# Polysketch attention and a mixture of experts: the expert stage in written order, with conditionals behind block 34

## The chip, the cores and the metric

The kernel runs on one core of a Trainium2 chip. The core has five engines with instruction queues of their own: TensorE (PE; its weight loads are listed as PEld), VectorE (DVE), ScalarE (ACT), GpSimd (POOL) and SyncE (SP). The metric is the time of one execution on the device in microseconds (us), as the median of several runs.

## What is computed

```python
# attention: phi(x) = (S1 x) (S2 x)^T, flattened
q_p, k_p = (phi(q), phi(k))                       # 4 batches, 4 heads, 1088 rows, 32 wide
kv = np.einsum('bhsf,bhsd->bhfd', k_p, v)
z = np.sum(k_p, axis=2)
x = einsum(q_p, kv) / (einsum(q_p, z) + 1e-06)    # -> x: 4352 tokens of 128
# mixture of experts behind two gates: 4 groups of 4 experts
g_idx = np.argmax(x @ w_group, axis=1)            # a token's group, weight g_w
e_idx = np.argmax(xg @ w_expert[g], axis=1)       # its expert in the group, weight e_w
h = np.maximum(xg[mask_e] @ w1[g, e], 0.0)        # 128 -> 1024
ye = h @ w2[g, e]                                 # 1024 -> 128
out[tok_idx] = (g_w * e_w)[:, None] * ye
```

The inputs come from a random generator with a fixed seed.

## The kernel before

The program has four stages. The first two read the keys and values and then the queries, and write the tokens x to DRAM as `x_d`. The third (routes) finds each token's expert and weight and sorts the tokens by expert into blocks of 128 slots: a block belongs to one expert, so an expert with 200 tokens takes two blocks. Any routing fits into `NBLK` = 49 blocks, and 34 is the least that 4352 tokens can fill. The routing leaves four tables in SBUF: `idx_g` (the row of `x_d` to fetch for each slot; 0 for an empty slot), `idx_s` (the row of the output to write; out of range for an empty slot, so that nothing is written), `wslot` (a slot's weight) and `bex` (a block's expert). `last` holds how many blocks end at each expert, so its last entry is the count of blocks that hold a token.

The fourth stage, on which the change bears, runs over all 49 blocks b, filled or not. For each block:

- `first_layer(b)`, lines 650 to 669: POOL gathers 128 rows of `x_d` into `xg` (an indirect DMA, L652). PE and DVE load the block's expert number from `bex` into a register (L655). DVE copies that expert's first weights out of `W1` into `w1b` (L658). PE transposes `xg` into PSUM (`pt`, L660) and DVE copies it to `xb` (L662). PE multiplies by the 8 pieces of `w1b` into `ph` (L665); in fp32 the trace shows two passes for each piece, 16 in all. ACT applies the relu and writes `hT` (L668).
- `second_layer(b)`, lines 671 to 682: PE multiplies the 8 pieces of `hT` by the expert's second weights into `py` (L674), again 16 passes, each piece with a register instruction before it (ISA in the lists below). DVE scales by `wslot` into `yo` (L678). POOL scatters `yo` to the output rows (an indirect DMA, L680). Since the rows are known only at run time, each scatter waits until the one before has landed.

The loop is written with the first layer one block ahead of the second. The order on each engine, however, is not the written one: the scheduler of the programming layer reorders the instructions by its own model of time, and buffers are handed out from pools (`xg` 4 buffers, `w1b`, `xb`, `hT`, `yo` 3, the PSUM tiles 2). The scheduler also splits the eight pieces of `py` around other work on PE.

Of the kernel before, what the change touches and what calls it, by code (L numbers as in the profile page):

```python
"""Polysketch attention, then a mixture of experts behind two gates: one core, one launch.

The reference's attention runs in float64 (its sketches S1, S2 come in float64), and its
quotient num / den is large just where den cancels. The chip's widest type is fp32, so den is
computed in parts: an operand is cut into bf16 slices on a fixed grid, products of slices are
summed on the tensor engine within 24 bits, and the sums of one order stay apart until the end.
  den[t] = sum_i a[t, i] c[t, i],  a = S1 q,  c = N q,  N = S1 G (S2^T S2),  G = sum_s k_s k_s^T
The numerator, the quotient and the experts are in fp32.

Tokens are then sorted by expert into blocks of 128 slots. NBLK blocks hold any routing. A  # L10
block picks its expert's weights, which stay in SBUF, by a register.
"""

# [9 lines left out]
F32 = mybir.dt.float32  # L23
BF16 = mybir.dt.bfloat16
I32 = mybir.dt.int32
ALU = mybir.AluOpType
ACT = mybir.ActivationFunctionType
AX = mybir.AxisListType
ENG = mybir.EngineType
PSUM = bass.MemoryType.PSUM  # L30
# [5 lines left out]
DM = H * D  # L36
N = B * S
# [3 lines left out]
G, EG, DFF = 4, 4, 1024  # L41
NE = G * EG
FC = DFF // 128
NBLK = (N - NE) // 128 + NE
NL = G + NE
NS = 4
# [7 lines left out]
def segments(c):  # L54
    """Token tile c: (batch, first row, rows)."""
    out, t = [], 128 * c
    while t < 128 * (c + 1):
        b = t // S
        e = min(128 * (c + 1), S * (b + 1))
        out.append((b, t - 128 * c, e - t))  # L60
        t = e
    return out
# [3 lines left out]
def attention_then_moe(ctx: ExitStack, tc: tile.TileContext, qT_d, kT_d, kn_d, vn_d, sT_d, s2_d,  # L66
                       wr_d, w1_d, w2_d, out):
    nc = tc.nc
# [3 lines left out]
    x_d = dram.tile([N, DM], F32, name="x_d")  # L72

    def kept(name, shape, dt=F32):
        return keep.tile(shape, dt, name=name)

    ident = kept("ident", [128, 128])
# [3 lines left out]

# [1 line left out]
    sT_i = kept("sT_i", [128, 2 * R, 2], I32)  # L83
# [7 lines left out]
    def power_above(m, n, psum, name):  # L91
        """[128, n] of maxima by partition -> a power of two above each column's, everywhere."""
        t = psum.tile([128, 256], F32, name="pw_t", tag="small")
# [15 lines left out]
    def grid(out, in_, c):  # L109
        """in_ rounded to a multiple of the last bit of c."""  # L110
        nc.vector.tensor_scalar(out=out, in0=in_, scalar1=c, scalar2=c, op0=ALU.add,  # L111
                                op1=ALU.subtract)
# [10 lines left out]
    def slices(dst, hi, lo, r):  # L123
        """hi + lo, hi below 1 and lo below its last bit, cut into dst [p, NS, n]; r is scratch."""
        rest = hi
        for i in range(NS):
            grid(dst[:, i], rest, ROUND * WQ[i])
            if i < NS - 1:
                sub(r, rest, dst[:, i])
                rest = r  # L130
                if i == 1:
                    add(r, r, lo)

    def products(out, left, right):
        """Sums of slice products by order: out(i) views orders i.., right(n) the first n slices."""
        for i in range(NS):
            nc.tensor.matmul(out(i), lhsT=left(i), rhs=right(NS - i), start=(i == 0),  # L137
                             stop=(i == NS - 1), skip_group_check=True)

# [1 line left out]
    def decode(w, p, n, tag):  # L141
# [50 lines left out]

# [1 line left out]
    with ExitStack() as kctx:  # L194
# [37 lines left out]

        # The sketches' slices, below 1, and Bm = S2^T S2.
        m1 = tiny.tile([128, 1], F32, name="m1")
# [17 lines left out]
        def refine(orders, n, name):  # L252
            """orders, sums [128, n] by order -> slices of their sum over a power of two."""
            o = [kbig.tile([128, n], F32, name=f"o{i}_{name}") for i in range(len(orders))]
            for t, z in zip(o, orders):
                nc.vector.tensor_copy(out=t, in_=z)
            hi, lo, t, u = (kbig.tile([128, n], F32, name=f"{x}_{name}") for x in "hltu")
            # hi + lo is the sum, and hi its nearest fp32.
            add(hi, o[0], o[1])
# [10 lines left out]
            hi = t  # L270
# [78 lines left out]

        # N = S1 G Bm, transposed: Bm (G S1^T).  # L350
        Gs, p_g = refine([Go[:, i].rearrange("p b d -> p (b d)") for i in range(NS + 1)], B * 32, "g")
# [27 lines left out]

# [1 line left out]
    with ExitStack() as qctx:  # L381
# [3 lines left out]
        def features(c0):  # L385
            """The parts of den before their last sums, and phi(q)."""
            nt = min(4, NT - c0)
# [116 lines left out]

# [1 line left out]
    idx_g = kept("idx_g", [128, NBLK], I32)  # L506
    idx_s = kept("idx_s", [128, NBLK], I32)
    wslot = kept("wslot", [128, NBLK])
    bex = kept("bex", [1, NBLK], I32)
    with ExitStack() as rctx:  # L510
        rp = rctx.enter_context(tc.tile_pool(name="rp", bufs=1, reuse_waits="tile"))
# [24 lines left out]
        def gate(z, k):  # L536
            """One-hot of the first largest of 4 logits, and the sum of the exponentials."""
            top = T(f"gt{k}", [NT])
# [28 lines left out]

        # Tokens of the same expert before a token: in its tile, and in the tiles before.
        lower, ones16 = T("lower", [128], BF16), T("ones16", [128], BF16)
# [48 lines left out]

        # A block's expert: how many experts end at it or before.
        le, bf = rp.tile([1, NBLK, NE], F32, name="le"), rp.tile([1, NBLK], F32, name="bf")  # L620
# [4 lines left out]

        # A slot's token and weight: one-hots of its place and its block, multiplied.
        in_b, vals = T("in_b", [NT, NBLK]), T("vals", [NT, 2, NBLK])
# [17 lines left out]

# [1 line left out]
    mp = ctx.enter_context(tc.tile_pool(name="mp", bufs=3, reuse_waits="tile"))  # L647
    mps = ctx.enter_context(tc.tile_pool(name="mps", bufs=2, reuse_waits="tile", space=PSUM))

    def first_layer(b):  # L650
        xg = mp.tile([128, DM], F32, name="xg", bufs=4)
        nc.gpsimd.indirect_dma_start(  # L652
            out=xg, out_offset=None, in_=x_d,
            in_offset=bass.IndirectOffsetOnAxis(ap=idx_g[:, b:b + 1], axis=0))
        ev = nc.values_load(bex[0:1, b:b + 1], engines=[ENG.PE, ENG.DVE], min_val=0, max_val=NE - 1,  # L655
                            skip_runtime_bounds_check_because="at most NE - 1, by a minimum")
        w1b = mp.tile([128, DFF], F32, name="w1b")
        nc.vector.tensor_copy(out=w1b, in_=W1[:, ds(ev, 1), :].rearrange("p o f -> p (o f)"))  # L658
        pt = mps.tile([128, DM], F32, name="pt")
        nc.tensor.transpose(pt, xg, ident)  # L660
        xb = mp.tile([128, 128], F32, name="xb")
        nc.vector.tensor_copy(out=xb, in_=pt)  # L662
        ph = mps.tile([128, FC, 128], F32, name="ph")
        for f in range(FC):
            nc.tensor.matmul(ph[:, f], lhsT=w1b[:, 128 * f:128 * f + 128], rhs=xb, start=True,  # L665
                             stop=True)
        hT = mp.tile([128, FC, 128], F32, name="hT")
        nc.scalar.activation(out=hT, in_=ph, func=ACT.Relu)  # L668
        return ev, hT

    def second_layer(b, ev, hT):
        py = mps.tile([128, DM], F32, name="py")
        for f in range(FC):
            nc.tensor.matmul(py, lhsT=hT[:, f],  # L674
                             rhs=W2[:, ds(ev * FC + f, 1), :].rearrange("p o d -> p (o d)"),
                             start=(f == 0), stop=(f == FC - 1))
        yo = mp.tile([128, DM], F32, name="yo")
        nc.vector.tensor_scalar(out=yo, in0=py, scalar1=wslot[:, b:b + 1], scalar2=None,  # L678
                                op0=ALU.mult)
        nc.gpsimd.indirect_dma_start(  # L680
            out=out, out_offset=bass.IndirectOffsetOnAxis(ap=idx_s[:, b:b + 1], axis=0), in_=yo,
            in_offset=None, bounds_check=N - 1, oob_is_err=False)

    ahead = first_layer(0)
    for b in range(NBLK):
        mine = ahead
        if b + 1 < NBLK:
            ahead = first_layer(b + 1)
        second_layer(b, *mine)

# [42 lines left out]
```

## Time and profile before

| | us |
|---|---|
| median of 3 runs | 509.83 |
| lowest and highest run | 509.80, 511.18 |
| span of the profiled execution, first to last instruction | 507.7 |
| PE busy in it | 402.5 (79%) |
| POOL busy | 208.2 (41%) |
| DVE busy | 253.8 (50%) |
| ACT busy | 73.0 (14%) |
| expert stage, from the first transpose of a gathered tile to the end | 298.3 to 507.7 |

The span is the profiled execution's own time between its first and its last instruction; what a run takes beyond it lies around the program. All times below are counted from the start of the span. A line of the kernel is written L674; an arrow `out<-in` names the tiles; `x49` is a count. In a timeline and in the chain of waits each row begins with a start and a duration in us, and brackets tell how long the engine had been idle and who ended that. Rows with a q behind the engine's name (POOLq, PEldq) are instructions of its queue, such as waits, register loads and drains; their durations are in ns.

### The profile page before, as it was taken

How to read it: one execution, taken by the hardware profiler on the slowest of the kernel's cores; microseconds unless marked ns; L12 is line 12 of the kernel's file. 1: busy time of each engine (PE TensorE's matmuls, PEld its weight loads, DVE VectorE, ACT ScalarE, POOL GpSimd, SP SyncE). 2: the span in 40 equal slices, each digit the busy share in tenths (PEclk: the TensorE clock that was granted, in tenths of full speed). 3: DMA queues.
4: the chain of work that ended last, by engine and by line, in shares of the span. 5: the costliest groups of instructions: out<-in, count | busy, mean ns of one | idle time of the engine just before them, and what ended most of it. 6: DMA issues, size and time to landing. Idle time of an engine off the chain costs nothing.

```text
span 507.7 us, 7633 instructions
## 1 busy us (share of the span) xinstructions
PE 402.5 (79%) x2724; PEld 331.7 (65%) x2724; DVE 253.8 (50%) x772; ACT 73.0 (14%) x104; POOL 208.2 (41%) x262
## 2 busy tenths in 40 slices
PE   0347979925899989997730659999999999999990
PEld 0326767812535638575620649999999999999980
DVE  8798363567645566655469932333233322233310
ACT  1000000001011111110110002322223222322220
POOL 0463163001735666535410053555554555455420
PEclk9998688956656565556555669999999999999996
DMA  8990482097000000000100010111111111111100
GB/s 304 374 250 1 156 254 64 0 354 308 2 1 21 22 21 23 20 22 0 43 11 0 0 33 25 32 34 28 29 34 37 28 32 34 35 31 26 12 1 0
DMA packets 16547, 34.28 MB, mean 68 GB/s; under 512 B 2597, under 2 KB 6961, under 8 KB 16512
## 3 DMA queue, kind: packets, MB, share of 16 engines
q1 hardware_dynamic: 13376, 28.35, 16.5%
q0 software_dynamic: 3136, 5.45, 4.6%
q8 instruction: 23, 0.38, 0.3%
q14 instruction: 12, 0.10, 0.1%
HBM read 29.33 MB, written 5.44 MB: 68 GB/s over the span
## 4 chain that ended last, share of the span: by engine, by line
PE 63%; DVE 18%; issue 6%; POOL 6%; ACT 3%; DMA 2%; POOLq 0%; SPq 0%; ACTq 0%; DVEq 0%
PE ph L665 17%; PE py L674 16%; PE ab L448 8%; PE pnum L475 5%; PE py L137 4%; PE pg L303 3%; ACT hT L668 3%; PE pl L491 2%; PE slot L637 2%; POOL rk L298 2%; DVE ks L111 2%; PE px L486 1%; POOL rq L396 1%; DVE top_p_k L89 1%; DVE kp L324 1%
## 5 line engine op out<-in xcount | busy, mean ns | idle before, releaser
L674 PE MATMUL py<-W,hT 128*128 x784 | 107.1, 281 | 2.7 <-ACT hT L668 2.6
L674 PEld LDWEIGHTS py<-W,hT 128*128 128x128 f32 x784 | 94.9, 192 | 11.5 <-ACT hT L668 11.5
L665 PE MATMUL ph<-xb,w1b 128*128 128x128 f32 x784 | 97.9, 280 | 0.0
L665 PEld LDWEIGHTS ph<-xb,w1b 128*128 128x128 f32 x784 | 94.0, 197 | 0.1
L652 POOL DMA_INDIRECT xg<-x_d,idx_g x49 | 49.7, 1014 | 107.2 <-PE pt L660 58.4
L668 ACT ACTIVATE hT<-ph 128x1024 f32<-128x1024 f32 x49 | 50.2, 1025 | 177.8 <-issue 111.3
L658 DVE COPY w1b<-W 128x1024 f32 x49 | 34.4, 705 | 74.7 <-issue 52.2
L680 POOL DMA_INDIRECT out_dram<-yo,idx_s x49 | 49.5, 1011 | 36.6 <-issue 12.5
L448 PE MATMUL ab<-qT,SR 64*128 64x512 f32 (+1 forms) x72 | 54.3, 999 | 0.1
L678 DVE TENSOR_SCALAR yo<-py,wslot 128x128 f32<-128x128 f32 x49 | 17.2, 351 | 62.5 <-PE py L674 62.0
L303 PE MATMUL pg<-ks 128*128 128x512 bf16 (+3 forms) x144 | 33.1, 348 | 16.8 <-DVE ks L111 16.8
L137 PEld LDWEIGHTS <-qs 128*128 128x128 bf16 (+1 forms) x144 | 14.9, 137 | 34.8 <-DVE qs L111 12.0
L137 PE MATMUL py<-M,qs 128*128 128x256 bf16 (+6 forms) x144 | 25.0, 322 | 9.9 <-DVE qs L111 7.0
L475 PE MATMUL pnum<-KV,qp 128*128 128x64 f32 (+1 forms) x144 | 30.7, 395 | 0.0
L475 PEld LDWEIGHTS pnum<-KV,qp 128*128 128x128 f32 (+1 forms) x144 | 28.8, 304 | 2.3 <-issue 1.5
L396 POOL TENSOR_TENSOR rq<-qT,qs 128x512 f32<-128x512 f32 (+1 forms) x9 | 10.1, 1122 | 48.9 <-DVE qs L111 42.3
L303 PEld LDWEIGHTS <-ks 128*128 128x128 bf16 x144 | 14.7, 112 | 21.4 <-issue 18.6
L111 DVE TENSOR_SCALAR qs<-rq,CQ 128x512 bf16<-128x512 f32 (+1 forms) x27 | 17.1, 633 | 21.9 <-POOL rq L396 21.9
L298 POOL TENSOR_TENSOR rk<-rk,ks 128x1152 f32<-128x1152 f32 x8 | 19.6, 2446 | 19.2 <-DVE ks L111 7.1
L448 PEld LDWEIGHTS ab<-qT,SR 64*128 64x128 f32 x72 | 16.5, 297 | 12.4 <-issue 6.9
L637 PE MATMUL slot<-vals,place 128*128 128x98 f32 x68 | 10.2, 325 | 15.1 <-DVE vals L518 15.1
L298 POOL TENSOR_TENSOR rk<-kn,ks 128x1152 f32<-128x1152 f32 x4 | 10.1, 2520 | 29.3 <-DVE pw L98 16.6
(312 smaller groups left out, 497.3 us busy)
## 6 DMA issues: line engine op xcount, KB each, us to landing
W<-in_w_dram SPq DMA_DIRECT2D x4, 2048.0 KB, 13.7
kn<-in_kn_dram SPq DMA_DIRECT2D x4, 576.0 KB, 5.8
kT<-in_kT_dram SPq DMA_DIRECT2D x4, 576.0 KB, 6.8
vn<-in_vn_dram SPq DMA_DIRECT2D x4, 576.0 KB, 4.0
qT<-in_qT_dram SPq DMA_DIRECT2D x4, 544.0 KB, 11.5
x_d<-xt SPq DMA_DIRECT2D x8, 256.0 KB, 2.2
xg<-x_d,idx_g POOLq DMA_INDIRECT x49
out_dram<-yo,idx_s POOLq DMA_INDIRECT x49
```

The source lines that it names most:

```text
L111: nc.vector.tensor_scalar(out=out, in0=in_, scalar1=c, scalar2=c, op0=ALU.add, op1=ALU.subtract)
L137: nc.tensor.matmul(out(i), lhsT=left(i), rhs=right(NS - i), start=(i == 0), stop=(i == NS - 1), skip_group_check=True)
L298: nc.gpsimd.tensor_tensor(out=r, in0=rest, in1=ks[:, i], op=ALU.subtract)
L303: nc.tensor.matmul(pg[:, i:NS, :], lhsT=ks[:, i, c, :], rhs=ks[:, 0:NS - i, c, :], start=(c == 0 and i == 0), stop=(c == SC - 1 and i == N ...
L448: nc.tensor.matmul(ab[x][:, 0:w], lhsT=SR[rows, x].rearrange("p a x y -> p (a x y)"), rhs=qf[rows], start=True, stop=True)
L475: nc.tensor.matmul(pnum[r0:r0 + n, c, 64 * pr:64 * pr + 64], lhsT=qp[:, pr, cols], rhs=KV[:, b, pr, :], start=True, stop=True)
L652: nc.gpsimd.indirect_dma_start(out=xg, out_offset=None, in_=x_d, in_offset=bass.IndirectOffsetOnAxis(ap=idx_g[:, b:b + 1], axis=0))
L658: nc.vector.tensor_copy(out=w1b, in_=W1[:, ds(ev, 1), :].rearrange("p o f -> p (o f)"))
L665: nc.tensor.matmul(ph[:, f], lhsT=w1b[:, 128 * f:128 * f + 128], rhs=xb, start=True, stop=True)
L668: nc.scalar.activation(out=hT, in_=ph, func=ACT.Relu)
L674: nc.tensor.matmul(py, lhsT=hT[:, f], rhs=W2[:, ds(ev * FC + f, 1), :].rearrange("p o d -> p (o d)"), start=(f == 0), stop=(f == FC - 1))
L680: nc.gpsimd.indirect_dma_start(out=out, out_offset=bass.IndirectOffsetOnAxis(ap=idx_s[:, b:b + 1], axis=0), in_=yo, in_offset=None, bounds ...
```

## The change

The two functions of the expert stage become five (`gather`, `weights`, `turn`, `first_layer`, `second_layer`), and a `step(b)` calls them for blocks b + 4, b + 2, b + 1, b + 2 and b, in this order. The stage is traced inside a block that keeps the written order on every engine, with tiles that are used in fixed rotation (6 of `xg`, 3 of the other SBUF tiles, 2 of the PSUM tiles, as many PSUM tiles as before). Steps 0 to 33 stand in a straight line. Step 34 and each later one stands in a conditional `tc.If(used > b)`, and each conditional stands inside the one before, so that the first one that does not hold leaves all the rest out. `used` is the count of blocks that hold a token, copied to an integer by DVE and loaded into a register by all five engines. The docstrings and comments are dropped as well, and the other stages stay as they are.

```diff
+LOW = N // 128
+TAIL = 1
...
+    n_used = kept("n_used", [1, 1], I32)
...
+        nc.vector.tensor_copy(out=n_used, in_=last[0:1, NE - 1:NE])
...
+    xg, w1b = ring(mp, "xg", [128, DM], 6), ring(mp, "w1b", [128, DFF], 3)
+    xb, hT = ring(mp, "xb", [128, 128], 3), ring(mp, "hT", [128, FC, 128], 3)
+    yo = ring(mp, "yo", [128, DM], 3)
+    ph, pt = ring(mps, "ph", [128, FC, 128], 2), ring(mps, "pt", [128, DM], 2)
+    py = ring(mps, "py", [128, DM], 2)
...
+    def turn(b):
+        if b >= NBLK:
+            return
+        nc.tensor.transpose(pt(b), xg(b), ident)
+        nc.vector.tensor_copy(out=xb(b), in_=pt(b))
...
-    ahead = first_layer(0)
-    for b in range(NBLK):
-        mine = ahead
-        if b + 1 < NBLK:
-            ahead = first_layer(b + 1)
-        second_layer(b, *mine)
+    def step(b):
+        gather(b + 4)
+        weights(b + 2)
+        first_layer(b + 1)
+        turn(b + 2)
+        second_layer(b)
+
+    def rest(b):
+        with tc.If(used > b):
+            for c in range(b, b + TAIL):
+                step(c)
+            if b + TAIL < NBLK:
+                rest(b + TAIL)
+
+    with tc.manual_schedule():
+        used = nc.values_load(n_used, min_val=LOW, max_val=NBLK,
+                              skip_runtime_bounds_check_because="LOW to NBLK, by construction")
+        for b in range(4):
+            gather(b)
+        for b in range(2):
+            weights(b)
+            turn(b)
+        first_layer(0)
+        for b in range(LOW):
+            step(b)
+        rest(LOW)
```

PE in the middle of the stage, before. Here `ph_2976` is a block's first layer, and `hT_2985` is what ACT makes of it; `py_2987` belongs to the block before. Five pieces of `py_2987` stand between the two, of which the first row is shown:

```order
L665 MATMUL ph_2976<-xb_2974,w1b_2970 128x128 x8
L674 ISA
L674 MATMUL py_2987<-W2_134,hT_2948 128x128
L655 TENSOR_LOAD bex_2071
...
L660 MATMUL pt_3009<-ident_64,xg_3001 128x128
L674 ISA
L674 MATMUL py_3024<-W2_134,hT_2985 128x128
...
L665 MATMUL ph_3013<-xb_3011,w1b_3007 128x128 x8
```

The same place in the changed kernel, one step with its end and the start of the next (the number behind a name is its place in the rotation; all eight pieces of `py1` and of `py0` stand together, of which one is shown):

```order
L699 MATMUL py1_2337<-W2_134,hT2_2328 128x128
L677 TENSOR_LOAD bex_2071
L693 MATMUL ph1_2333<-xb1_2324,w1b1_2321 128x128 x8
L686 MATMUL pt0_2334<-ident_64,xg2_2316 128x128
L699 ISA
L699 MATMUL py0_2336<-W2_134,hT0_2326 128x128
```

On PE the last two pieces of work for a block have moved apart: between a `ph` and the `py` that reads its `hT` there now stand a transpose, the whole `py` of the block before, the `ph` of the next block and another transpose.

POOL late in the stage, before, where gathers (L652) and scatters (L680) alternate until the gathers run out:

```order
L652 DMA xg_4037<-x_d_63,idx_g_2068 128x128
L680 DMA out_0_dram<-yo_3884,idx_s_2069 4352x128
L652 DMA xg_4074<-x_d_63,idx_g_2068 128x128
L680 DMA out_0_dram<-yo_3921,idx_s_2069 4352x128
L680 DMA out_0_dram<-yo_3958,idx_s_2069 4352x128
...
L680 DMA out_0_dram<-yo_4120,idx_s_2069 4352x128
L729 UNCONDITIONAL_BRANCH
```

POOL in the changed kernel, from the last step of the straight part into the first conditionals:

```order
L670 DMA xg1_2315<-x_d_63,idx_g_2068 128x128
L704 DMA out_0_dram<-yo0_2329,idx_s_2069 4352x128
L716 COMPARE_AND_BRANCH
L670 DMA xg2_2316<-x_d_63,idx_g_2068 128x128
L704 DMA out_0_dram<-yo1_2330,idx_s_2069 4352x128
```

A branch now stands behind each scatter from block 33 on, and the same stands on PE, DVE, ACT and SP after their share of a step. On the side that is taken when a condition does not hold, POOL first waits for its transfers and raises the counts of the semaphores that the skipped steps would have raised, and then jumps to the end of the program.

## Rows read from the trace of the kernel before

**Rows 1.** The page: span of the profiled execution.

```profile
span 507.7 us, 7633 instructions
```

**Rows 2.** Stages: us from:to, busy PE, PEld, DVE, ACT, POOL; PEclk, DMA, GB/s.

```profile
275.00:285.00 10.00, 1.90 (x9) 1.90 (x10) 9.86 (x22) 0.00 (x0) 0.00 (x0) 0.50 0.00 0
...
330.70:435.50 104.80, 104.52 (x887) 99.53 (x887) 32.37 (x79) 27.01 (x27) 53.59 (x54) 1.00 0.12 32
...
435.50:495.70 60.20, 57.87 (x485) 54.30 (x483) 17.32 (x42) 15.02 (x15) 25.99 (x25) 1.00 0.13 20
```

**Rows 3.** Timeline of the stage's start: DVE's first copies, PE's first work.

```profile
294.66 1.90 DVE L658 COPY w1b<-W 128x1024 f32 x3 [0.55 <-DVE idx_s L518]
...
298.25 0.48 PE L660 MATMUL pt<-ident,xg 128*128 128x128 f32 x1 [4.97 <-DMA xg<-x_d,idx_g]
...
300.06 6.16 PE L665 MATMUL ph<-xb,w1b 128*128 128x128 f32 x32
```

**Rows 4.** Chain of waits, mid stage: start, us, what.

```profile
402.11 1.79 PE ph L665 x16
403.89 1.12 PE py L674 x10
405.01 0.11 PE pt L660
405.12 0.89 PE py L674 x6
```

**Rows 5.** Waits from 308 to 495.7: us in total, times, longest.

```profile
PEld py L674 <- ACT hT L668: 11.5, 43, 0.5
```

**Rows 6.** Timeline, PE late in the stage.

```profile
443.82 0.27 PE L660 MATMUL pt<-ident,xg 128*128 128x128 f32 x1
...
444.27 1.16 PE L674 MATMUL py<-W,hT 128*128 x8 [0.17 <-ACT hT L668]
...
447.94 0.27 PE L660 MATMUL pt<-ident,xg 128*128 128x128 f32 x1
```

**Rows 7.** Timeline, mid stage: DVE, ACT and POOL in one block.

```profile
396.13 0.70 DVE L658 COPY w1b<-W 128x1024 f32 x1 [2.23 <-issue]
...
396.19 1.03 ACT L668 ACTIVATE hT<-ph 128x1024 f32<-128x1024 f32 x1 [2.87 <-issue]
...
397.60 0.99 POOL L652 DMA_INDIRECT xg<-x_d,idx_g  x1 [1.61 <-PE pt L660]
...
398.89 1.00 POOL L680 DMA_INDIRECT out_dram<-yo,idx_s  x1 [0.30 <-issue]
```

**Rows 8.** Stages again: traffic (last column, GB/s) late in the stage.

```profile
440.00:460.00 20.00, 19.32 (x164) 18.22 (x163) 6.39 (x15) 4.52 (x6) 10.35 (x10) 1.00 0.20 33
...
460.00:480.00 20.00, 19.15 (x163) 17.96 (x162) 6.21 (x15) 4.78 (x5) 9.63 (x9) 1.00 0.14 17
```

**Rows 9.** Timeline, the last two blocks on DVE and POOL.

```profile
493.45 0.35 DVE L678 TENSOR_SCALAR yo<-py,wslot 128x128 f32<-128x128 f32 x1 [3.57 <-PE py L674]
...
494.07 0.98 POOL L680 DMA_INDIRECT out_dram<-yo,idx_s  x1 [3.14 <-DVE yo L678]
...
495.78 0.35 DVE L678 TENSOR_SCALAR yo<-py,wslot 128x128 f32<-128x128 f32 x1 [1.98 <-PE py L674]
...
497.84 0.98 POOL L680 DMA_INDIRECT out_dram<-yo,idx_s  x1 [2.79 <-DMA out_dram<-yo,idx_s]
```

**Rows 10.** Chain of waits at the end: a scatter from start to landing.

```profile
489.96 2.09 DMA out_dram<-yo,idx_s
```

**Rows 11.** Queue instructions of L729: ns min/median/max, first and last start.

```profile
L729 POOLq DRAIN  x3: 40/107/9283, 497.6 to 507.4; - x3
...
L729 PEldq DRAIN  x2: 13/489/965, 494.8 to 507.2; - x2
```

**Rows 12.** DMA: a code queue's packets, MB, share; smallest load's us to landing.

```profile
q8 instruction: 23, 0.38, 0.3%
...
sT_i<-in_sT_dram SPq DMA_DIRECT2D x1, 16.0 KB, 1.6
```

More of the change, by code (lines that the diff above doesn't have):

```diff
@@ L644, in attention_then_moe @@
         tt(idx_s, tk, none, ALU.add)
-    mp = ctx.enter_context(tc.tile_pool(name="mp", bufs=3, reuse_waits="tile"))
-    mps = ctx.enter_context(tc.tile_pool(name="mps", bufs=2, reuse_waits="tile", space=PSUM))
-    def first_layer(b):
[L651 to L663, printed above, removed]
+    mp = ctx.enter_context(tc.tile_pool(name="mp", bufs=1, reuse_waits="tile"))
@@ new lines, in attention_then_moe, with ring @@
+    mps = ctx.enter_context(tc.tile_pool(name="mps", bufs=1, reuse_waits="tile", space=PSUM))
+    def ring(pool, name, shape, n):
+        tiles = [pool.tile(shape, F32, name=f"{name}{i}") for i in range(n)]
+        return lambda b: tiles[b % n]
+    xg, w1b = ring(mp, "xg", [128, DM], 6), ring(mp, "w1b", [128, DFF], 3)
+    xb, hT = ring(mp, "xb", [128, 128], 3), ring(mp, "hT", [128, FC, 128], 3)
+    yo = ring(mp, "yo", [128, DM], 3)
+    ph, pt = ring(mps, "ph", [128, FC, 128], 2), ring(mps, "pt", [128, DM], 2)
@@ new lines, in attention_then_moe, with gather, weights @@
+    py = ring(mps, "py", [128, DM], 2)
+    ex = {}
+    def gather(b):
+        if b >= NBLK:
+            return
+        nc.gpsimd.indirect_dma_start(
+            out=xg(b), out_offset=None, in_=x_d,
+            in_offset=bass.IndirectOffsetOnAxis(ap=idx_g[:, b:b + 1], axis=0))
+    def weights(b):
+        if b >= NBLK:
+            return
+        ex[b] = nc.values_load(bex[0:1, b:b + 1], engines=[ENG.PE, ENG.DVE], min_val=0,
+                               max_val=NE - 1,
+                               skip_runtime_bounds_check_because="at most NE - 1, by a minimum")
+        nc.vector.tensor_copy(out=w1b(b),
+                              in_=W1[:, ds(ex[b], 1), :].rearrange("p o f -> p (o f)"))
@@ L664, in first_layer @@
+    def turn(b):
+        if b >= NBLK:
+            return
+        nc.tensor.transpose(pt(b), xg(b), ident)
+        nc.vector.tensor_copy(out=xb(b), in_=pt(b))
+    def first_layer(b):
+        if b >= NBLK:
+            return
         for f in range(FC):
-            nc.tensor.matmul(ph[:, f], lhsT=w1b[:, 128 * f:128 * f + 128], rhs=xb, start=True,
+            nc.tensor.matmul(ph(b)[:, f], lhsT=w1b(b)[:, 128 * f:128 * f + 128], rhs=xb(b), start=True,
                              stop=True)
-        hT = mp.tile([128, FC, 128], F32, name="hT")
@@ L668, in first_layer, with second_layer @@
[L668 to L672, printed above, removed]
+        nc.scalar.activation(out=hT(b), in_=ph(b), func=ACT.Relu)
+    def second_layer(b):
         for f in range(FC):
-            nc.tensor.matmul(py, lhsT=hT[:, f],
-                             rhs=W2[:, ds(ev * FC + f, 1), :].rearrange("p o d -> p (o d)"),
+            nc.tensor.matmul(py(b), lhsT=hT(b)[:, f],
+                             rhs=W2[:, ds(ex[b] * FC + f, 1), :].rearrange("p o d -> p (o d)"),
@@ L676, in second_layer @@
                              start=(f == 0), stop=(f == FC - 1))
-        yo = mp.tile([128, DM], F32, name="yo")
-        nc.vector.tensor_scalar(out=yo, in0=py, scalar1=wslot[:, b:b + 1], scalar2=None,
+        nc.vector.tensor_scalar(out=yo(b), in0=py(b), scalar1=wslot[:, b:b + 1], scalar2=None,
                                 op0=ALU.mult)
         nc.gpsimd.indirect_dma_start(
-            out=out, out_offset=bass.IndirectOffsetOnAxis(ap=idx_s[:, b:b + 1], axis=0), in_=yo,
+            out=out, out_offset=bass.IndirectOffsetOnAxis(ap=idx_s[:, b:b + 1], axis=0), in_=yo(b),
```

## Prediction

> **What bounds the kernel now.** I read the page first: one execution spans 507.7 us [rows 1]. The stage table comes next. From 306.2 us to the end the program is the expert stage, and from 330.7 to 435.5 TensorE is busy for 104.5 of 104.8 us at a granted clock of 1.00; from 435.5 to 495.7 it is 57.9 of 60.2 [rows 2]. DVE (17.3 us of those 60.2), ACT (15.0) and POOL (26.0) are far from full, so TensorE sets the pace, and what can be gained is its number of blocks and its gaps.
>
> The chain of waits in the middle of the stage shows one block: 16 matmul passes ph (1.79 us), 10 passes py (1.12), one transpose pt (0.11), 6 passes py that take 0.89 us, then the next ph [rows 4]. Ten passes in 1.12 us are 0.112 us each, so six should take 0.67; the other 0.22 us is a wait. The view of waits names it: PE's weight load for py waits for ACT's hT 43 times, 11.5 us in all [rows 5]. hT takes 1.03 us after ph [rows 7], and the old order puts only 10 + 1 passes (1.23 us) between the last ph and the first py that needs its hT. So a block costs 16 + 16 + 1 passes = 1.79 + 1.79 + 0.11 = **3.69 us of work**, and 3.90 us with the wait. Later the old order puts only 8 + 1 passes there and PE waits longer: pt starts at 443.82 and py at 444.27, 0.45 us later where 0.11 would do, and the next pt starts at 447.94 [rows 6]: a block takes 4.12 us there.
>
> **How many blocks are skipped.** The inputs are fixed by the seed of the reference. Routing them by the reference gives 16 experts 188 to 399 tokens each; rounded up to blocks of 128 these are 40 filled blocks of 49. The traffic agrees: 33 GB/s (gather and scatter) up to 460 us, 17 GB/s from 460 to 480 [rows 8], while POOL goes on issuing both; the scatters that carry nothing begin there, and the fortieth block ends there. So used = 40: the conditionals for blocks 34 to 39 are entered, the one for block 40 is not, and blocks 41 to 48 are never begun. Block 40's first layer and the transposes of blocks 40 and 41 are still done, because step 39 runs them ahead.
>
> **The change part by part.**
>
> *Start.* In both versions the order of PE is pt, pt, ph, ph. The new loads of n_used stand on every engine's queue; on DVE one more load stands before the first w1b copy. That copy started at 294.66 after a gap of 0.55 us, most of it such a load, while the first gathered tile reached PE at 298.25 [rows 3]: hidden by over 2 us; without that cover it would cost up to 0.55. The two first-layer groups ended at 300.06 + 6.16 = 306.2 [rows 3] and I keep that. The CAST that makes n_used sits in DVE's routing chain, which is full (9.86 of 10 us for 22 instructions [rows 2]): between 0 and 9.86/22 = 0.45 us; one element is nearer the small end, so +0.15.
>
> *Expert steps.* From 306.2 the new stream on PE is pt and py of step 0 (0.11 + 1.79 = 1.90), then 39 steps of 16 + 1 + 16 passes, 3.69 us each if nothing waits: 306.2 + 1.9 + 39 x 3.69 = **452.0**. Before, the last py ended at 495.6 (its DVE reader starts at 495.78 [rows 9]). That is 43.6 us less. By cause: 8 x 16 ph + 7 pt + 9 x 16 py = 279 passes removed, x 0.112 = 31.2 us, and 12.4 us of gaps. Does anything wait in the new order? py(b) follows ph(b+1), pt, and the sixteen passes of py(b-1) came before, so hT(b) has 3.7 us for its 1.03. For ph(b+2), DVE must do yo(b-1) (0.35 [rows 9]), w1b(b+2) (0.70 [rows 7]) and the load (0.55 at most [rows 3]), some 1.6 us after py(b-1), and the copy xb(b+2) about 0.5 us after pt(b+2), which is 1.90 into the step; it is done at 2.4 of 3.69. POOL does a gather (0.99) and a scatter (1.00) per step, 1.29 apart from start to start [rows 7], and each scatter waits for the landing of the one before, about 2.1 us after its start [rows 10]: some 2.9 us per step, and nothing on PE waits for it closely, as gathers run four blocks ahead. If that cover fails, PE takes POOL's pace; the rival below prices it.
>
> *Six entered conditionals.* Each engine has one COMPARE_AND_BRANCH per conditional, with no join of engines in the built program. No row shows such an instruction here. From below it costs nothing: PE's queue had been issued 0.96 us before its end when its sequencer reached the drain [rows 11], so anything shorter is hidden. From above it is a fetch of code each time: a block of code takes 24.4/23 = 1.06 us to move (0.3% of 16 engines' 507.7 us by 23 packets [rows 12]), and the smallest load needs 1.6 us from issue to landing [rows 12]; 1.6 + 1.06 - 0.96 = 1.7 us for six, 10 us. I take 0: the entered block stands right behind the branch, and no wait of PE in the stage is put down to code, though its code came in such packets all along [rows 5, 12].
>
> [...] No row of before shows a branch either way.
>
> *End.* Before, the last scatter started at 497.84, 2.06 us after its yo started, since it waited for the landing of the scatter before; the one ahead of it needed 494.07 - 493.45 = 0.62 [rows 9]. In the new order two scatters are 3.69 us apart, so 0.62 holds: -1.4 us. Then comes POOL's drain of 9.28 us [rows 11], which began with the last scatter; from that scatter's start to the end of the span are 507.7 - 497.84 = 9.86 us. Now POOL leaves by the false side of the conditional for block 40, which first waits for all its transfers (2.1 us after the scatter's start) and adds one instruction for semaphore counts, and only then drains. If the drain ends when it would have anyway: +0. If it takes its 9.28 us from the later start: +2.7. If it was only waiting for transfers: about -6. I take +1.3. PE, DVE and ACT also jump to the false side; a fetch there (at most 2.7 us) lies under POOL's drain.
>
> **Sum.** 507.7 - 43.6 - 1.4 + 1.3 + 0.15 = 464.2 us of span. The median of the runs is 509.83, 2.13 over the span; the same on top: **466.3 us**.
>
> **Rivals.**
> *A: the fixed order finds its own wait and a block stays at 3.90.* For: two scatters that follow each other only by landing were 497.84 - 494.07 = 3.77 us apart [rows 9], more than 3.69. Against: the scatter before those landed after 2.09 [rows 10], and 2.9 us a step would then do. Price 39 x 0.21 = 8.2: 474.5.
> *B: entered conditionals stall the engines.* Six times 0.6 to 1.7 us beyond PE's lead, 4 to 10 us; at 6, 472.3. For: PE's code moves in few large packets [rows 12]. Against: the target is next in line. [...]
> *C: the drain was only waiting for transfers.* 466.3 - 1.3 - 6 = 459. Against: the drain ran on for some 7 us after the last landing.
> *D: nothing is skipped* (the count is 49, or the branch never leaves): 49 blocks at 3.69, 308.1 + 48 x 3.69 = 485.2 for PE, with 12.1 for the end, 0.15 and 2.1 above the span 499.5.
> *E: every conditional joins the engines as the end of the program does.* The nearest row is that end, 9.86 us from POOL's last scatter: 6 x 9.86 = 59, so 525, slower than before. It decides from (509.8 - 466.3)/6 = 7.25 us per conditional. Against: only branches stand there.
>
> **How the numbers follow.** Chances: forecast 0.62, A 0.10, B 0.15, C 0.06, D 0.03, E 0.04. The forecast's own range is 463.5 to 469 (drain, n_used, small gaps). To leave out no more than 2 in 10 the range runs from 462.5 to 474.5: it takes in B's middle and A's value, and leaves C, D, E and the far side of A and B. A measurement can tell 0.3% from no change (1.5 us): faster 0.96 (all but E), same 0.01 and slower 0.03 (E, if its price is near or over 7.25).
>
> **What would show it.** In the changed profile: PE's waits for hT gone and hT's neighbours 3.69 us apart; 40 scatters and 44 gathers; last py near 452; POOL's drain starting 2 to 3 us behind the last scatter. A pace of 3.9 means A; gaps of PE only at the six branches mean B; a scatter count of 49 means D. The forecast is wrong above all if the drain's length follows something else, or if PE cannot run 40 blocks without a gap.

## The result and the profile after

The changed kernel takes **468.78 us** (median of four runs, lowest 467.57, highest 469.38). The kernel before, run beside it, takes 510.5. The ratio is 0.918 with a 95% interval of 0.9155 to 0.9205. The forecast was 466.3 with a range of 462.5 to 474.5: the direction and most of the sum were right, and 2.5 us are missing.

Stage table of the changed kernel, columns as in [rows 2], and the start of the page:

```profile
span 465.7 us, 6912 instructions
```

```profile
306.20:330.70 24.50, 24.50 (x222) 24.50 (x222) 8.78 (x21) 6.95 (x7) 14.71 (x13) 1.00 0.11 31
330.70:435.50 104.80, 104.80 (x942) 104.80 (x941) 38.42 (x86) 29.22 (x29) 64.48 (x57) 1.00 0.12 34
435.50:452.00 16.50, 15.96 (x144) 15.77 (x142) 5.70 (x13) 4.55 (x5) 10.98 (x9) 1.00 0.20 38
452.00:465.70 13.70, 0.00 (x0) 0.00 (x0) 0.00 (x0) 0.00 (x0) 1.02 (x1) 0.62 0.06 9
```

PE now has 942 passes in the middle stretch where it had 887 [rows 2], and its weight loads are busy for the whole of it (99.5 of 104.8 us before). No wait of PE stands in the stage any more; the 43 waits for hT [rows 5] are gone. One step, from PE's timeline:

```profile
425.52 1.95 PE L693 MATMUL ph<-xb,w1b 128*128 128x128 f32 x16
427.31 0.27 PE L686 MATMUL pt<-ident,xg 128*128 128x128 f32 x1
427.42 1.95 PE L699 MATMUL py<-W,hT 128*128 x16
429.20 1.95 PE L693 MATMUL ph<-xb,w1b 128*128 128x128 f32 x16
```

From ph to ph is 429.20 - 425.52 = 3.68 us, and PE's first branch (427.2, next rows) falls into this step. The branches themselves, in the view of the line of the conditionals (L716; ns min/median/max, first and last start in us):

```profile
L716 PEldq COMPARE_BRANCH  x8: 65/69/3317, 427.2 to 453.0; - x8
L716 DVEq COMPARE_BRANCH  x8: 43/43/67, 429.4 to 452.3; - x8
L716 POOLq COMPARE_BRANCH  x8: 34/34/50, 429.8 to 457.8; - x8
L716 POOLq EVENT_SEMAPHORE  x4: 17/43/2182, 453.4 to 455.8; - x4
L716 POOLq INC_SWDGE_SEM  x1: 1860/1860/1860, 455.9 to 455.9; - x1
```

Entered branches take 0.03 to 0.07 us, PE's first 0.095. The long ones belong to the branch that leaves: PE's of 3.3 us, and on POOL a wait of 2.18 us for the last scatter to land and 1.86 us for INC_SWDGE_SEM, which by its place raises the counts of the skipped transfers. Then comes the final drain (first row of it below), and, in POOL's timeline, the last two scatters with the last gather between them:

```profile
L773 POOLq DRAIN  x3: 40/107/6933, 457.9 to 465.4; - x3
```

```profile
448.45 1.52 POOL L704 DMA_INDIRECT out_dram<-yo,idx_s  x1 [0.87 <-DVE yo L702]
450.28 0.97 POOL L670 DMA_INDIRECT xg<-x_d,idx_g  x1 [0.31 <-issue]
453.13 1.02 POOL L704 DMA_INDIRECT out_dram<-yo,idx_s  x1 [1.88 <-DMA out_dram<-yo,idx_s]
```

The last yo started at 451.50, so the last scatter came 1.63 us behind it, held by the landing of the scatter before. From that scatter to the end of the span are 465.7 - 453.13 = 12.57 us; before they were 9.86.

### The profile page after: what moved, and what is told of

Read it like the earlier page. It is cut to its first block, busy times and chain, and to the rows that moved or that the text cites. A ratio compares the mean times of both kernels' runs of the same rounds, so it can differ in the third digit from the quotient of the medians.

```text
span 465.7 us, 6912 instructions
## 1 busy us (share of the span) xinstructions
PE 362.4 (78%) x2445; PEld 299.8 (64%) x2445; DVE 248.1 (53%) x750; ACT 64.7 (14%) x96; POOL 205.9 (44%) x248
## 4 chain that ended last, share of the span: by engine, by line
PE 54%; DVE 20%; issue 11%; POOL 9%; DMA 2%; ACT 0%; SPq 0%; POOLq 0%; DVEq 0%; ACTq 0%
PE ph L693 12%; PE py L699 11%; PE ab L450 9%; PE pnum L477 5%; PE py L139 4%; PE pg L305 3%; PE pl L493 3%; POOL xg L670 3%; PE slot L642 2%; POOL rk L300 2%; DVE ks L113 2%; PE px L488 1%; POOL rq L398 1%; DVE top_p_k L91 1%; DVE kp L326 1%
## 5 line engine op out<-in xcount | busy, mean ns | idle before, releaser
L693 PE MATMUL ph<-xb,w1b 128*128 128x128 f32 x656 | 82.5, 281 | 0.0
L693 PEld LDWEIGHTS ph<-xb,w1b 128*128 128x128 f32 x656 | 79.3, 198 | 0.0
L699 PE MATMUL py<-W,hT 128*128 x640 | 78.0, 275 | 0.0
L704 POOL DMA_INDIRECT out_dram<-yo,idx_s x40 | 53.2, 1331 | 49.3 <-DVE yo L702 31.4
L699 PEld LDWEIGHTS py<-W,hT 128*128 128x128 f32 x640 | 74.6, 192 | 0.0
L670 POOL DMA_INDIRECT xg<-x_d,idx_g x44 | 43.7, 992 | 52.2 <-DVE idx_s L521 39.1
L695 ACT ACTIVATE hT<-ph 128x1024 f32<-128x1024 f32 x41 | 42.0, 1023 | 143.2 <-PE ph L693 135.2
L702 DVE TENSOR_SCALAR yo<-py,wslot 128x128 f32<-128x128 f32 x40 | 14.0, 351 | 59.9 <-PE py L699 52.5
L680 DVE COPY w1b<-W 128x1024 f32 x42 | 29.4, 700 | 8.3 <-DVE yo L702 5.0
L687 DVE COPY xb<-pt 128x128 f32<-128x128 f32 x42 | 12.2, 291 | 33.8 <-PE pt L686 29.6
L450 PEld LDWEIGHTS ab<-qT,SR 64*128 64x128 f32 x72 | 16.7, 299 | 12.4 <-issue 7.0
## 6 DMA issues: line engine op xcount, KB each, us to landing
W<-in_w_dram SPq DMA_DIRECT2D x4, 2048.0 KB, 12.4
```

The lines of the kernel that those rows point to most:

```text
L450: nc.tensor.matmul(ab[x][:, 0:w], lhsT=SR[rows, x].rearrange("p a x y -> p (a x y)"), rhs=qf[rows], start=True, stop=True)
L670: nc.gpsimd.indirect_dma_start(out=xg(b), out_offset=None, in_=x_d, in_offset=bass.IndirectOffsetOnAxis(ap=idx_g[:, b:b + 1], axis=0))
L680: nc.vector.tensor_copy(out=w1b(b), in_=W1[:, ds(ex[b], 1), :].rearrange("p o f -> p (o f)"))
L693: nc.tensor.matmul(ph(b)[:, f], lhsT=w1b(b)[:, 128 * f:128 * f + 128], rhs=xb(b), start=True, stop=True)
L695: nc.scalar.activation(out=hT(b), in_=ph(b), func=ACT.Relu)
L699: nc.tensor.matmul(py(b), lhsT=hT(b)[:, f], rhs=W2[:, ds(ex[b] * FC + f, 1), :].rearrange("p o d -> p (o d)"), start=(f == 0), stop=(f == ...
```

## The experiments

All times are medians, each beside runs of the kernel before on the same chip (510.0 to 510.3 us there). Three runs beside the changed kernel's make a table of two by two and one more:

| | 49 blocks | 40 blocks | 40 by conditionals |
|---|---|---|---|
| scheduler's order | 510.0 (before) | 471.92 | not run |
| written order | 496.46 | 463.75 | 468.78 (changed) |

**Only the order.**

```diff
-        for b in range(LOW):
+        for b in range(NBLK):
             step(b)
-        rest(LOW)
```

> The changed kernel's written order and rotating tiles, but all 49 steps in a straight line, no conditional: only the order is new, nothing is skipped. Theory (a step takes 3.68 us of TensorE when py no longer waits for hT, and the skipped passes are worth the rest): the last py ends 8 x 3.68 + 1.79 = 31.2 us later than the 451.5 us of the changed kernel, at 482.7; last scatter about 0.6 after its yo, then 9.9 us to the end of the span as before: 493.6 span, 495 to 497 us. So the order alone gives about 14 us of the 42. Rival (the order is worth nothing by itself, the whole gain is skipping): 510 us.

Measured: 496.46 us, ratio 0.974 (0.9707 to 0.9774), as the theory said. The order alone is worth 13.5 us with 49 blocks.

**Only the skipping.**

```diff
-    for b in range(NBLK):
+    for b in range(40):
         mine = ahead
```

> The kernel before with its scheduler's order, its loop cut from 49 to 40 blocks (the nine blocks of empty slots are left out; a straight line, no conditional): only the skipping is new. Theory: 279 passes fewer, 31.2 us, and the waits for hT stay (0.21 to 0.43 us in a block, some 10 us in all): 474 to 479 us, hT waits still in the view of waits. Rival (the waits for hT come from the empty blocks or the end only, so that 40 blocks run at 3.69): 467 us.

Measured: 471.92 us, ratio 0.9256 (0.9225 to 0.9287), below the expected range and far from the rival's 467. The waits view, from 308 to 461 us (total, times, longest):

```profile
PEld py L674 <- ACT hT L668: 7.7, 36, 0.4
```

The waits for hT stay with the old order. Skipping alone is worth 38.1 us. That is 31.2 for the passes, about 9 x 0.43 = 3.9 for the waits of nine blocks late in the stage, where a block took 4.12 us instead of 3.69 [rows 6], and some 2.8 at the end that I had left out of the expectation: the last scatter starts 0.63 us behind its yo (460.20 - 459.57) instead of 2.06, and the final drain is 1.4 us shorter (9.28 to 7.91).

**Order and skipping without conditionals.**

```diff
-        for b in range(LOW):
+        for b in range(40):
             step(b)
-        rest(LOW)
```

> The changed kernel with exactly 40 steps in a straight line and no conditional (blocks 40 to 48 left out by the loop's bound): its difference to the changed kernel is what six entered conditionals and the one that is left cost. Theory (entered ones cost nothing, the false side moves POOL's drain back by about 2.7 us): 465 to 467 us, 2 to 3 us under the changed kernel, no INC_SWDGE_SEM of 1.9 us at the end, and the last scatter still 1.6 us behind its yo. Rival 1 (the drain ends when it would have anyway): the same time, 468.8. Rival 2 (the entered conditionals cost as well): more than 4 us under it.

Measured: 463.75 us, ratio 0.9096 (0.906 to 0.9133): 5.0 us under the changed kernel. By time alone this is rival 2's number, but the trace has the theory's place: PE's last yo starts at 451.45, as in the changed kernel (451.50), so nothing is lost in the steps. All of it lies behind, in the last scatter, which I had expected to be held here too, and in the false side, which is dearer than the 2.7 us of the theory. POOL's timeline and its drain:

```profile
448.82 1.02 POOL L704 DMA_INDIRECT out_dram<-yo,idx_s  x1 [0.82 <-DVE yo L702]
450.15 0.97 POOL L670 DMA_INDIRECT xg<-x_d,idx_g  x1 [0.30 <-issue]
452.07 1.02 POOL L704 DMA_INDIRECT out_dram<-yo,idx_s  x1 [0.96 <-DVE yo L702]
```

```profile
L772 POOLq DRAIN  x3: 40/113/8190, 451.8 to 460.6; - x3
```

The last scatter starts 0.62 us behind yo, not 1.63: 1.06 us earlier on the time axis of the trace (453.13 - 452.07). The drain does its work from the end of that scatter (453.09) to 460.03, 6.94 us; in the changed kernel it starts 4.78 us after the scatter's start, behind the wait for the landing and INC_SWDGE_SEM, instead of 1.02: 3.76 us. 1.06 + 3.76 = 4.8, the difference of the two spans.

**Forty entered conditionals.**

```diff
-LOW = N // 128
+LOW = 0
```

> The changed kernel with conditionals from block 0 on: 40 entered instead of 6. Theory (an entered branch takes 0.03 to 0.07 us of an engine's queue and no code has to be awaited): within 1 us of the changed kernel. Rival (0.6 to 1.7 us for each beyond PE's lead, as my prediction's rival B priced it): 34 more, 20 to 58 us longer, with gaps of PE at each branch.

Measured: 470.29 us, ratio 0.9217 (0.918 to 0.9254): 1.5 us more for 34 more branches, 0.04 us each, far under rival B's 20, and the two intervals overlap. Even this does not lie at the branches: PE is busy for 104.80 of 104.80 us from 330.7 to 435.5 here too. In this kernel POOL's drain begins 2.7 us after its last branch (461.08, the branch at 458.36).

```profile
L716 PEldq COMPARE_BRANCH  x42: 65/65/3457, 299.9 to 453.6; - x42
L773 POOLq DRAIN  x3: 40/107/7016, 461.1 to 468.7; - x3
```

**The distance from ph to py.**

```diff
+        second_layer(b)
         first_layer(b + 1)
         turn(b + 2)
-        second_layer(b)
```

> The changed kernel with each step's py put ahead of the next block's ph: on PE the stream is ph(b), pt, py(b), so one pass (0.11 us) instead of 34 stands between a ph and the py that reads its hT. Theory (the gap of the old order is hT's 1.02 us and its two hand-overs, less what stands between; 0.21 us were left with 11 passes, 1.23 us, so the whole way is about 1.45): 1.45 - 0.11 = 1.3 us more in each of 40 blocks, 468.8 + 53 = 520, PE waiting for hT some 40 times. Rival (the old waits came from something else, the ACT queue or the loads): under 490.

Measured: 518.32 us, ratio 1.0168 (1.0134 to 1.0201), slower than before although nine blocks are skipped. The waits view from 300 us on:

```profile
PEld py L699 <- ACT hT L695: 50.8, 39, 1.5
```

50.8/39 = 1.30 us for each block, the expected number, and the rival's time is far off. In these runs the wait for hT follows the distance in PE's order between a ph and its py: 1.30 us a block with one pass between, 0.43 with nine and 0.21 with eleven [rows 4, 6], none with 34.

**The drain.** The kernels so far suggested that the final drain goes by the count of indirect DMAs. A drain put into the stage, where POOL has time, should then shorten the last one.

```diff
         second_layer(b)
+        if b % 4 == 1:
+            nc.gpsimd.drain()
```

> The changed kernel with a drain of POOL behind the scatter of every fourth step (1, 5, ... 33, 37). The final drains measured so far are proportional to the indirect DMAs of the program: 98 give 8.08 us behind POOL's last work (before and s49), 84 give 6.93 to 6.94 (changed kernel, s40), 81 give 6.69 (old40), 0.0825 us for each. Theory (a drain works off the DMAs issued since the last one): each of the new ones takes some 0.7 us beside PE's work, the final one 4 x 0.08 = 0.3, so the time falls by 6.6 to 462; if INC_SWDGE_SEM (1.86 us) also walks the same DMAs, by up to 8.4 to 460.4. Rival (the final drain has its length whatever was drained, or goes by all DMAs of the program): 468.8, or slower where POOL's waits reach PE.

```diff
+        if b == 21:
+            nc.gpsimd.drain()
```

> The changed kernel with one added drain of POOL behind step 21. 48 of the 84 indirect DMAs are issued by then. Theory: this drain takes 48 x 0.0825 = 4.0 us, the final one 36 x 0.0825 = 3.0 instead of 6.9, the time falls by 4 to some 465 (half of INC_SWDGE_SEM's 1.9 may go too); PE sees nothing of it, as gathers run four blocks ahead. Rival (fixed length): 468.8.

Measured: **461.23 us**, ratio 0.9044 (0.901 to 0.9078), and 464.32 us, ratio 0.9103 (0.9075 to 0.913). The rival falls in both. The rows of the added drains, of INC_SWDGE_SEM and of the final drains, first with a drain behind every fourth step, then with the single one:

```profile
L715 POOLq DRAIN  x10: 2775/2874/5139, 312.1 to 446.0; - x10
...
L718 POOLq INC_SWDGE_SEM  x1: 260/260/260, 457.8 to 457.8; - x1
...
L775 POOLq DRAIN  x3: 46/107/382, 458.2 to 459.4; - x3
```

```profile
L715 POOLq DRAIN  x1: 5687/5687/5687, 385.9 to 385.9; - x1
...
L718 POOLq INC_SWDGE_SEM  x1: 900/900/900, 457.0 to 457.0; - x1
...
L775 POOLq DRAIN  x3: 46/107/3005, 458.1 to 461.7; - x3
```

The final drain follows the DMAs issued since the last one, and so does INC_SWDGE_SEM:

| kernel | indirect DMAs not yet drained | final drain, us | INC_SWDGE_SEM, us |
|---|---|---|---|
| changed | 84 | 6.933 | 1.860 |
| room for 41 blocks (below) | 81 | 6.684 | 1.807 |
| one drain behind step 21 | 36 | 3.005 | 0.900 |
| every fourth step to 33 (below) | 12 | 1.035 | 0.420 |
| every fourth step to 37 | 4 | 0.382 | 0.260 |
| every step (below) | 0 | 0.055 | 0.185 |

That is (6.933 - 0.382)/80 = 0.082 us for each DMA in the drain and (1.860 - 0.260)/80 = 0.020 in the other. The drains in the middle were taken for shorter than they are: 2.87 us where 0.7 was expected. They begin while the scatter before them is still on its way (the last from 446.0 on, that scatter on POOL from 446.27 to 447.29), and the next kernel shows what they wait for.

```diff
         second_layer(b)
+        nc.gpsimd.drain()
```

> The changed kernel with a drain of POOL behind the scatter of every step. Theory: a drain of two DMAs takes 0.2 us, POOL has room for it in its 3.69 us, final drain 0.2 us: 460 to 462. Rival (a drain also waits until the scatter has landed, some 1.2 us after its descriptors are written): POOL's step of 1.5 + 1.2 + 1.0 and two gaps of 0.3 is then over 3.69, PE falls to POOL's pace, 4 to 4.5 us a block, 475 or more.

Measured: 497.64 us, ratio 0.974 (0.971 to 0.9771): the rival was right. The waits view from 300 us on:

```profile
POOL xg L670 <- DMA out_dram<-yo,idx_s: 64.7, 30, 3.2
...
PEld pt L686 <- DMA xg<-x_d,idx_g: 31.5, 34, 1.7
```

These drains also wait until what is on its way has landed: the last three in the steps end 0.12 us after the last piece of the scatter before them. One per step makes POOL's step about 4.5 us, over PE's 3.68, and PE waits for gathered tiles. One in four steps is nearly made up for in the other three: from the first ph to the last yo are 152.7 us with it, 152.5 with the single drain and 152.0 in the changed kernel, so the drains cost PE 0.5 to 0.7 us, where the expectation had none.

**Why the last scatter is held.**

> The changed kernel with the empty slots of a block gathering 128 different rows (row p in partition p) instead of row 0 for all; one more small DVE instruction in the routing. It asks why the scatter of step 38 landed 3.88 us after its start in the changed kernel (2.1 before), which held the last scatter back by 1.0 us. Theory (a 16 KB packet of code, fetched for PE's leaving branch from 450.3 on, held up one of the DMA engines): no change, 468.5 to 469.2, the landing still late. Rival (the gather of an empty block, 128 times the same row, stood in its way): landing after 2.3, and 1 us less, 467.8.

```diff
-        nc.vector.tensor_scalar(out=idx_g, in0=tk, scalar1=0.0, scalar2=None, op0=ALU.max)
+        own = T("own", [NBLK])
+        nc.vector.tensor_scalar(out=own, in0=none, scalar1=tok1[:, 0:1], scalar2=1.0 / BIG,
+                                op0=ALU.mult, op1=ALU.mult)
+        tt(idx_g, tk, own, ALU.add)
```

Measured: 468.49 us, ratio 0.9182 (0.9156 to 0.9207), no change, and the late landing stays. Last row of the chain of waits, with spread rows and then in the changed kernel:

```profile
450.10 3.53 DMA out_dram<-yo,idx_s
```

```profile
448.45 3.88 DMA out_dram<-yo,idx_s
```

So it is not the gather of one row 128 times. The theory's other half was tried by a shorter way out:

```diff
-NBLK = (N - NE) // 128 + NE
+NBLK = 41
```

> The changed kernel with room for 41 blocks instead of 49: blocks 41 to 48, which stand unreached in the code and which step 39 partly gathers ahead, are left out. The leaving branch then jumps over one step of code, not nine. Theory (PE's fetch of far code holds up one DMA engine, so that the scatter of step 38 lands 1.0 to 1.2 us late and holds the last scatter back): PE's leaving branch takes well under 3.3 us, the scatter of step 38 lands after 2.1 to 2.5 us, the last scatter starts 0.6 to 0.9 after its yo; with three gathers fewer for the drain (-0.25): 467.3 to 467.8. Rival (the delay is of the scatters and gathers themselves): still 1.6 to 2.0 behind yo, 468.5.

Measured: 467.34 us, ratio 0.9169 (0.9148 to 0.9191), a time in the theory's range, but not for its reason. PE's leaving branch shrank to 0.36 us, but the delay did not go: the last scatter starts 2.17 us behind its yo (456.16 and 453.99).

```profile
L716 PEldq COMPARE_BRANCH  x8: 65/69/357, 429.8 to 454.1; - x8
...
L716 POOLq INC_SWDGE_SEM  x1: 1807/1807/1807, 456.1 to 456.1; - x1
```

What this kernel gained lies on the false side. Only one step is left out there, not nine, and POOL has no wait (EVENT_SEMAPHORE) among its rows of L716, where the changed kernel has four. INC_SWDGE_SEM starts together with the last scatter and the drain 1.96 us after the scatter's start (458.12 - 456.16), instead of 4.78. In the span this is hidden, since the last yo of this execution lies 2.5 us later than in the changed kernel.

A packet of code was fetched all the same, later. The DMA view between the last two scatters of this kernel (packets, MB, share of 16 engines), and of the changed kernel:

```profile
q8 instruction: 1, 0.02, 1.7%
```

```profile
q8 instruction: 1, 0.02, 1.3%
```

The late landings go with it. In the changed kernel the code packet runs from 450.31 to 451.31 and the scatter's last pieces land at 452.33; in this one it runs from 452.90 to 454.33 and the last piece lands at 455.36, 2.1 us after the other fifteen. Where no code packet falls between the last two scatters and the one before has time to land (40 blocks in a straight line, in either order), the last scatter starts 0.62 and 0.63 us behind its yo. The kernel with the distance of one pass has the same conditionals, but its code packet begins only at 504.79, behind the last scatter's start. There the scatter of step 38 lands after 2.30 us, and the last one starts 0.63 us behind its yo (504.08):

```profile
504.71 1.02 POOL L704 DMA_INDIRECT out_dram<-yo,idx_s  x1 [2.72 <-DVE yo L702]
```

The rest of the stage agrees. In the 14 traces together, 503 scatters have the landing of all 16 pieces on record, and in 65 of them the last piece comes over 0.4 us after the fifteenth. In 63 of these 65 a 16 KB code packet ran between the scatter's start and its landing, and the last piece landed 0.93 to 1.41 us after the packet's end. Such landings stand in the straight kernels too: in before, the last piece of the scatter at 494.07 came 0.89 us after the fifteenth and 1.18 us after the packet's end (495.90). What the conditionals add is the place: in the changed kernel PE's leaving branch starts at 449.31 and the packet 1.0 us later, while step 38's scatter is on its way. I hold the packet for the cause, by this agreement; no run changed the packet alone.

**What is left of the conditionals' price, and the last drain's place.**

> 40 steps in a straight line, no conditional, with a drain of POOL behind every fourth step: the bound of what the conditionals still cost once the drain is short. Theory: the final drain 0.3 instead of 6.9 us; the end is then the landing of the last scatter (2.2 us after its start) and the closing exchange of the engines: 457 to 458, some 4 us under the same with conditionals (waiting for the landing before the counts, the counts, the held-up scatter). Rival (with short drains nothing is left of the conditionals' price): 461.

The edit is the loop over 40 and the drain of every fourth step together. Measured: 460.95 us, ratio 0.9046 (0.9017 to 0.9076), which is the rival's number, but not for its reason. This execution's expert stage began two us late (first ph at 301.54, last yo at 453.53; 299.67 and 451.45 without drains), and its last scatter started 1.97 us behind that yo, at 455.51: POOL is behind after the drain of step 37. With these two the gain is eaten, and the medians do not settle what the conditionals cost once the drain is short. The two traces give a part of it: from the last scatter's start to the end of the span are 3.73 us here (459.24 - 455.51) and 5.06 with conditionals and the drain up to step 37 (459.67 - 454.61), so 1.3 us are left on the false side.

> The changed kernel with a drain of POOL behind every fourth step of the straight part alone (1, 5, ... 33), none in the conditionals. In the kernel with the drain behind step 37 as well, POOL was 1.6 us late after it and the last scatter started 2.3 us behind its yo. 12 of the 84 indirect DMAs are left for the end. Theory (the final drain takes 0.0825 us for each DMA not yet worked off; INC_SWDGE_SEM 0.18 + 0.02 for each): final drain 1.0 us, INC_SWDGE_SEM 0.42, last scatter 1.6 behind its yo as in the changed kernel: 468.8 - 5.9 - 1.4 = 461.5, or 460.5 if the starts agree with those of the kernel with the drain behind step 37. Rival (the nine added drains delay PE's or POOL's steps in the straight part): over 463.

```diff
+        if b % 4 == 1 and b < LOW:
+            nc.gpsimd.drain()
```

Measured: 463.45 us, ratio 0.9066 (0.9034 to 0.9098), runs from 461.27 to 465.47: by the median on the rival's side. The final drain (1.035) and INC_SWDGE_SEM (0.420) are as expected to 0.04 us. The last scatter starts not 1.6 but 3.1 us behind its yo (458.11 and 455.00): the one before it started 2.0 us behind its own, as POOL was still late, and took 3.99 to land, again beside a code packet. Besides, the profiled run is the slowest of the five, and it was late before the expert stage: the first ph starts at 301.36, against 299.52 in the changed kernel. In the stage from 70 to 130 us, which no edit touches, PE's granted clock was lower; this kernel first, then the changed one:

```profile
70.00:130.00 60.00, 41.92 (x324) 28.23 (x324) 37.44 (x143) 3.30 (x10) 12.75 (x8) 0.68 0.49 182
```

```profile
70.00:130.00 60.00, 40.12 (x330) 27.77 (x329) 36.83 (x144) 3.74 (x12) 12.54 (x8) 0.77 0.50 184
```

The rest fits the rival: from the first ph to the last yo are 153.6 us, against 152.0 in the changed kernel, and PE gets through 928 passes from 330.7 to 435.5 where it had 942. The intervals of the two drain versions overlap; which place is better is not settled. The one with a drain behind every fourth step up to 37 is, at 461.23 us, the fastest with conditionals that was run, 7.5 us under the changed kernel.

## Why the prediction was right, and where it missed

*PE's work.* Right. The step is 3.68 us where 3.69 was summed, the last py ends at 451.5 instead of 452.0. Half of the 0.5 us comes from the start, where the first two ph end at 305.95, not 306.2; the rest is 39 steps of a little under 3.69. In the changed kernel the first gather took POOL 1.18 us, against 1.85; DVE's copy of w1b began 0.22 us behind it (295.08 and 294.86), where in the kernel before it had begun 0.18 us ahead of it (294.66 and 294.84). I put the difference down to that. The added register load on DVE, which I had costed at 0 to 0.55, delayed that copy, and so turned into a gain: without that load (49 and 40 blocks in a straight line) the copy follows the routing's last instruction after 0.66 us instead of 0.96, and the gather takes 1.69.

*Passes skipped and gaps closed: 31.2 + 12.4.* Right. Order and skipping each gain by themselves: 13.5 and 8.2 us for the order (with 49 and with 40 blocks), 38.1 and 32.7 for the skipping (in the old and the new order). They overlap: 13.5 + 38.1 = 51.6, and both together give 46.3 (510.0 - 463.75). Some 3.9 of the 5.3 us between are the waits of the nine late blocks, which either of the two removes; the rest was not taken apart. The kernel with the distance of one pass shows that the gaps were put down to the right wait.

*Entered conditionals at 0.* Right; 34 more cost 1.5 us by the medians and leave no gap on PE. The six entered ones took 34 to 40 ns on POOL, 43 to 55 on DVE and 65 to 95 on PE, so they did not stall. PE's leaving branch took 3.3 us, and 0.36 where it jumped over one step of code; the 3.3 us lay under POOL's tail.

*Last scatter: -1.4.* **Wrong, the first step that failed.** I took the 2.06 us of before [rows 9] for two scatters too close together, and expected 0.62 once they were 3.68 apart. They were, and the scatter still waited 1.63. The landing had taken 3.88 us, not the 2.09 of [rows 10]. In before, the chain row of the scatter that held the last one shows 3.00 us, and a code packet ran from 494.62 to 495.90:

```profile
494.07 3.00 DMA out_dram<-yo,idx_s
```

[Rows 10] was the wrong scatter to read, the one before that. So 0.9 of the 2.06 us were the late landing (3.00 - 2.09), not the short distance. Missed: 1.0 us.

*POOL's drain: +1.3 between 0 and +2.7.* **Wrong in its make-up.** The tail grew by 12.57 - 9.86 = 2.7, the upper bound, but not as either bound had it. The drain itself shrank, from 98 DMAs to 84 (8.08 us behind the last scatter's own work to 6.93, -1.15). The false side cost 3.76 us, of which I had seen the wait for the landing and had taken INC_SWDGE_SEM for a mere count; it takes 1.86. Missed: 1.4 us. Rival C is refuted: in the changed kernel everything had landed 2 us before the drain began, and it took 6.93 all the same.

*The sum.* 464.2 - 0.7 (PE, n_used) + 1.0 + 1.4 = 465.9, and the profiled span is 465.7. That execution took 467.57, the least of the four; the median lies 1.2 higher. The other three executions had a lower mean granted clock (0.762 to 0.772, against 0.773); no trace of them shows more. 468.78 lies at the upper edge of the forecast's own range, 463.5 to 469; the wider range was drawn for rivals A and B, and neither came true.

*Rivals.* A fell (3.68, no wait of PE), though POOL's scatters grew from 1.01 to 1.33 us on average. B fell with the forty conditionals. D and E fell (40 scatters, no joins).

## What to carry to other kernels

The drain of POOL that closes this program was paid for each indirect DMA since the last one (0.082 us each): where POOL had idle time under PE's work, drains in the middle took it off the end at a small price (0.5 to 0.7 us of PE's time, 1.7 in the slowest trace), but one in every step made POOL the bound by its waits for landings (4.5 us a step against PE's 3.68). Count everything that stands on the side of a conditional that is not entered: here a wait of 2.18 us and INC_SWDGE_SEM's 1.86 us lay there, and at the end of the program they lay on the path. With one step skipped instead of nine, POOL did not wait there at all, and its drain began 1.96 us after the last scatter's start instead of 4.78. Before a landing time goes into a sum, take it from the transfer that releases the wait, not from its neighbour.

## What the runs showed that was not expected

The final drain took 0.082 us and INC_SWDGE_SEM 0.020 us for each indirect DMA issued since the last drain, in kernels with 0 to 84 of them, beside 0.055 and 0.185 us that stay when none is left. The drains in every step also waited for the landing of what was under way, and the last three ended 0.12 us after it.

POOL took longer over some indirect DMAs beside a DVE copy: 1.52 us for the scatter at 448.45 in the changed kernel, beside the w1b copy of 448.39 to 449.08, and 1.02 for the one at 448.82 in the straight 40 blocks, which started while no more than 0.13 us of that copy were left. Not over all: in the old order with 40 blocks the scatter at 451.96 took 0.98 us beside the copy of 451.94 to 452.68.

Some scatters beside a 16 KB packet of code landed their last piece late: 2.1 us after the other fifteen in the kernel with room for 41 blocks, and 0.93 to 1.41 us after the packet's end in 63 of the 65 late landings on record, some of them in straight kernels.
